# Order of the weight completion, pool order and operand temporaries in an attention and two-stage expert kernel on one core

## The chip, the cores and the metric

The kernel runs on one core of a Trainium2 chip. The metric is the device time of one execution, in microseconds (us). The core's engines are TensorE (PE, the matmuls), VectorE (DVE), ScalarE (ACT), GpSimd (POOL), and SyncE (SP), which here issues all DMAs in one queue, in order.

## The reference

Chunked attention with 8 memory slots, then two feed-forward stages on its 3072 output rows, all in fp32:

```
scores = scale * (q_c @ k_full.T); a = softmax(scores); x = a @ v_full      # B=4, H=8, S=768, D=64, chunks of 32
h = x @ w_in;  g = h * tanh(softplus(h));  x = g @ w_out                    # 3072x512 by 512x2048 by 2048x512
xn = x / sqrt(mean(x*x) + 1e-6) * rms_g
out = (silu(xn @ w_gate) * (xn @ w_val)) @ w_out2                           # 512x1536 twice, 1536x512
```

## The kernel before, in words

**Precision.** Every fp32 matrix is split into a high part and a low remainder. `split` (L145, L146) does it in two steps: ACT casts the high part (L145), then DVE subtracts it from the source (L146). Each product is then three matmuls (high by high, high by low, low by high: L612 to L614, L725 to L727, L854 to L856).

**Seven products for eight.** The stages w_in, gate/value and w_out2 form each 2x2 block product from seven products of sums of blocks, numbered 1 to 7 and run in the order 1, 6, 5, 4, 2, 7, 3 (`group`). Sums of the right operand's blocks are made on DVE in `sum_pieces` (L588 to L591, two of them into temporaries), then split one by one. Sums of a weight's blocks are made once: a weight of w_in that was first used with plain blocks is completed by `finish`, which adds high and low part back together on DVE (L273, two instructions for each weight), forms four sums on POOL (L278, L279) and DVE (L280, L281), and splits them into the remaining places of its slot.

**Stages.** Attention is interleaved with the w_in stage at the start: a block of 384 tokens that is ready is evacuated by ACT into `xb` (L516), and plain products of it (`unit`, evacuated by ACT at L662) keep PE busy until two blocks make a pair. From the second pair on the seven products are used. Results `g` go to `g_scratch` in HBM. The w_out stage reads `g_scratch` back through `Feed`: `load` brings a step's operand, `split` applies the activation (ACT, L753) and splits it; a step `s` calls `load(s+3)`, `split(s+3)`, `load(s+5)`. Three operands are split ahead of the loop. The weights of w_out arrive as raw fp32 (`raw`, L141) and are converted by ACT and DVE (L194, L197, L201, L202, L208). RMS normalisation and the gate/value stage (`group2`, results to `h_scratch`) follow, then the last stage, `group3`: 24 units (j, r), each of seven products of 18 matmuls with 256 columns. Its six weight slots `o2` are loaded by `w_load` (L124), its operands by `h_load` (L835) and `h_pieces`.

**Order.** A scheduler that simulates the program decides, from data dependences and buffers, in which order each engine's instructions stand; `pin` keeps an instruction in the order of the program text. Buffers come from pools that rotate. The pools `cp` (6 tiles of 1.5 KB for each partition), `gp` (5 of 3 KB) and `tp` (8 of 6 KB) are closed after the w_in stage, and the pools of the later stages, `gl` (4 KB), `c` (2 of 2 KB) and `t` (8 of 8 KB), take the same 72 KB. A late tile waits for whatever last used the bytes under it.

Where a row of the tables says `w`, `s`, `sm` or `raw`, it names the tile whose bytes are used, which can hold something else: the second unit's operands lie in weight slot 2 (`w<-h_scratch`).

Of the kernel before, what the change touches and what calls it, by code (L numbers as in the profile page):

```python
# [8 lines left out]
F32 = mybir.dt.float32  # L9
# [4 lines left out]
ALU = mybir.AluOpType  # L14
# [15 lines left out]
def tile_kernel(  # L30
# [15 lines left out]
    nc = tc.nc  # L46
# [36 lines left out]
    rawp = ctx.enter_context(tc.tile_pool(name="rawp", bufs=2))  # L83
    cap = ctx.enter_context(tc.tile_pool(name="cap", bufs=3))
    mid_stack = ExitStack()
    cp = mid_stack.enter_context(tc.tile_pool(name="cp", bufs=6))
    gp = mid_stack.enter_context(tc.tile_pool(name="gp", bufs=5))
    tp = mid_stack.enter_context(tc.tile_pool(name="tp", bufs=8))
    late_pools = {}
    psp = ctx.enter_context(tc.tile_pool(name="psp", bufs=1, space=bass.MemoryType.PSUM))  # L90
    bk = [psp.tile([128, 512], F32, name=f"bk{c}") for c in range(6)]
# [27 lines left out]
    def as7(s):  # L119
        return s.rearrange("p (a l f) -> p a l f", a=7, l=2)  # L120

    def w_load(key, u):
        s = w_slot(u)
        nc.sync.dma_start(out=s.bitcast(F32), in_=wd[key].bitcast(F32))  # L124
        wtab[key] = as7(s)

    def w_store(key, half):
# [140 lines left out]
    def finish(key):  # L268
        w = wtab[key]
        aa = [cap.tile([128, 512], F32, tag="ca", name="ca") for n in range(2)]  # L270
        for n, a in enumerate(aa):
            hi, lo = (w[:, 2 * n:2 * n + 2, l, :].bitcast(F32) for l in range(2))
            nc.vector.tensor_tensor(a.rearrange("p (a f) -> p a f", a=2), hi, lo, op=ALU.add)  # L273
        a0, a1 = aa
        a11, a12, a21, a22 = a0[:, 0:256], a0[:, 256:512], a1[:, 0:256], a1[:, 256:512]
        sm = cvp.tile([128, 4, 256], F32, tag="sm", name="sm")
        s4, s1, s2, s3 = (sm[:, i, :] for i in range(4))
        nc.gpsimd.tensor_tensor(s1, a21, a22, op=ALU.add)  # L278
        nc.gpsimd.tensor_tensor(s3, a11, a21, op=ALU.subtract)  # L279
        nc.vector.tensor_tensor(s2, s1, a11, op=ALU.subtract)  # L280
        nc.vector.tensor_tensor(s4, a12, s2, op=ALU.subtract)  # L281
        yield
        split(s4, w[:, 2, 0, :], w[:, 2, 1, :])
        yield
        split(sm[:, 1:4, :], w[:, 4:7, 0, :], w[:, 4:7, 1, :])
        yield
# [271 lines left out]
    def t_pieces(j, x0, x1, new, temp_new, dram, tab):  # L558

        return sum_pieces(j, x0[:, 0:2, :], x0[:, 2:4, :], x1[:, 0:2, :], x1[:, 2:4, :],  # L560
                          new, temp_new, dram, tab)

    def sum_pieces(j, b11, b21, b12, b22, new, temp_new, dram, tab):
        cols = b11.shape[2]
        size = b11.shape[1] * cols
        temp = {}

        def as_block(x):
            return x[:, 0:size].rearrange("p (a n) -> p a n", n=cols)

        def one(p, src):
            t = new()
            if isinstance(t, tuple):
                split(src, *t)
                for l in range(2):
                    store_later(dram[:, p - 1, l].bitcast(F32), t[l].bitcast(F32))
                return
            v = t.rearrange("p l a n -> p l (a n)")[:, :, 0:size]
            v = v.rearrange("p l (a n) -> p l a n", n=cols)
            split(src, v[:, 0], v[:, 1])  # L580
            if dram is not None:
                store_later(dram[:, p - 1].bitcast(F32), t.bitcast(F32))
            tab[j, p] = v

        def sums():
            for p in (2, 4):
                temp[p] = as_block(temp_new(p).rearrange("p a n -> p (a n)"))
            nc.vector.tensor_tensor(b11, b12, b11, op=ALU.subtract)  # L588
            nc.vector.tensor_tensor(temp[2], b22, b11, op=ALU.subtract)
            nc.vector.tensor_tensor(temp[4], temp[2], b21, op=ALU.subtract)  # L590
            nc.vector.tensor_tensor(b12, b22, b12, op=ALU.subtract)  # L591

        early = [lambda: one(1, b11), sums]
        rest = [lambda: one(6, temp[2]), lambda: one(5, b11), lambda: one(4, temp[4]),
                lambda: one(2, b21), lambda: one(7, b12), lambda: one(3, b22)]
        return early, rest

# [15 lines left out]
            nc.tensor.matmul(ps, whi, xl, start=False, stop=False, **more)  # L613
            nc.tensor.matmul(ps, wlo, xh, start=False, stop=kk == 1, **more)  # L614

    def group(mul, banks, n_, c12, c21, c22, temps):

        X, Y, Z, V = banks
        x, y, z, vv = (b_[:, 0:n_] for b_ in banks)
        s1, u2, z5 = temps()  # L620
        mul(1, X, True)
        nc.scalar.copy(s1, x)  # L622
        yield
        mul(6, Y, True)
        nc.vector.tensor_tensor(u2, y, s1, op=ALU.add)
        yield
        mul(5, Z, True)
        nc.scalar.copy(z5, z)
        yield
        mul(4, V, True)  # L630
        yield
        mul(2, X, False)
        yield
        mul(7, Y, False)
        u3 = s1
        nc.vector.tensor_tensor(u3, y, s1, op=ALU.add)  # L636
        yield
        mul(3, Z, False)
        nc.vector.tensor_tensor(c12, z, u2, op=ALU.add)
        nc.gpsimd.tensor_tensor(c22, u3, z5, op=ALU.add)  # L640
        nc.vector.scalar_tensor_tensor(
            c21, vv, -1.0, u3, op0=ALU.mult, op1=ALU.add
        )
        yield
# [194 lines left out]
        hraw[n] = parts  # L839

    def h_pieces(n):
        return sum_pieces(n, *hraw.pop(n), t_new2, v_temp, None, ttab_h)

    def group3(n, j, r, between):
        o = s_new()
        o = [o[:, a, :] for a in range(2)]

        def mul(p, bank_, first):
            t = ttab_h[n, p]
            ps = bank_[:, 0:256]  # L850
            more = dict(skip_group_check=not first)
            for f in range(HG):
                w = wtab["o2", f][:, W_AT[p]]
                nc.tensor.matmul(ps, t[:, 0, f], w[:, 0], start=first and f == 0, stop=False, **more)  # L854
                nc.tensor.matmul(ps, t[:, 0, f], w[:, 1], start=False, stop=False, **more)  # L855
                nc.tensor.matmul(ps, t[:, 1, f], w[:, 0], start=False, stop=f == HG - 1, **more)  # L856

        banks = group_banks(8)
        c11 = banks[0][:, 0:256]
        c12, c21, c22 = o[1][:, 0:256], o[0][:, 256:512], o[1][:, 256:512]  # L860
        run([group(mul, banks, 256, c12, c21, c22, lambda: (c_new()[:, 0:256], c12, c22))], between)
        nc.scalar.copy(o[0][:, 0:256], c11)
        for a in range(2):
            row = (2 * j + a) * N2 + 128 * r
            store_later(out[row:row + 128, :], o[a])
# [182 lines left out]
    late_pools["gl"] = late_pool("gl", 1)  # L1048
    late_pools["c"] = late_pool("c", 2)
    late_pools["t"] = late_pool("t", 8)  # L1050
    pend = []
    sq_new = lambda: [c_new() for _ in range(2)]
    for s, (m, i) in enumerate(steps):
# [106 lines left out]
    for jn, j in enumerate(jback):  # L1160
# [7 lines left out]
        for f in range(HG + 2 if jn else HG, F2):  # L1168
            run([group2(j, f)], preparing(0, bt) if last and f == F2 - 1 else bt)
            if last and f == HG + 2:  # L1170
                w_load(("o2", 3), 5)
            elif last and f == HG + 3:
                h_load(0, *units[0])
                w_load(("o2", 4), 6)
            elif last and f == HG + 4:
                w_load(("o2", 5), 3)
    h_load(1, *units[1])
    for n, (j, r) in enumerate(units):
        if 0 < n < len(units) - 1:
# [34 lines left out]
```

## Time and profile before

| | |
|---|---|
| median of the runs | 1191.08 us (1189.69 to 1196.43, 3 runs) |
| profiled execution | 1190.69 us, span 1188.9 us |
| mean granted clock of TensorE | 0.990 of full speed |
| busy: PE, DVE, ACT, POOL | 1153.8, 817.5, 621.5, 215.1 us |
| DMA, mean over the span | 247 GB/s |

The span runs from the first instruction to the last; the execution's own time holds the span and 1.8 us around it. Busy is the time in which an engine executes. PE's busy time includes stretches at the lower of its two clocks, so busy does not mean busy at full speed. An idle time is told with its releaser, the instruction whose end let the waiting one start.

### The profile page before, as it was taken

The page shows a single profiled execution, that of the slowest core. Times are in us where ns is not written, and L with a number is a line of the kernel's source. Part 1 is how long each engine was busy: PE and PEld are TensorE (multiplying, and loading weights), DVE is VectorE, ACT ScalarE, POOL GpSimd, SP SyncE. Part 2 cuts the span into 40 slices and gives each one's busy share as a digit, 9 for nine tenths or more (in the row PEclk, how much of TensorE's full clock was granted, in tenths as well). Part 3 has the DMA queues.
Part 4 walks back from the last instruction along what each step waited for, and adds up shares of the span by engine and source line. Part 5 has one row for each costly group of instructions (what it writes and reads, how often), then busy time and mean ns, then how long its engine had stood idle before and what let it go on. Part 6 is the DMA issues. An engine that isn't in the chain of part 4 may idle for free.

```text
span 1188.9 us, 22951 instructions
## 1 busy us (share of the span) xinstructions
PE 1153.8 (97%) x9052; PEld 1008.5 (85%) x9052; DVE 817.5 (69%) x1212; ACT 621.5 (52%) x996; POOL 215.1 (18%) x185
## 2 busy tenths in 40 slices
PE   6899899999999899999999999999999999999998
PEld 4789899999999688888878878878888888999998
DVE  4655898854755856675775675976886746887773
ACT  5566566543545866667665443553454423444442
POOL 2010222310132411030131121322221211000000
PEclk8899989999999999999999999999999999999999
DMA  9889869899488764595589388899889878654420
GB/s 188 172 230 217 209 239 264 231 293 300 148 304 289 246 204 129 187 362 163 195 329 393 144 343 333 321 416 391 319 312 377 315 264 293 195 173 142 142 90 36
DMA packets 219132, 294.20 MB, mean 247 GB/s; under 512 B 104208, under 2 KB 168720, under 8 KB 210064
## 3 DMA queue, kind: packets, MB, share of 16 engines
q1 hardware_dynamic: 219024, 292.73, 74.1%
q8 instruction: 71, 1.16, 0.4%
q14 instruction: 37, 0.30, 0.1%
HBM read 181.80 MB, written 110.89 MB: 246 GB/s over the span
## 4 chain that ended last, share of the span: by engine, by line
PE 74%; DMA 8%; DVE 7%; ACT 5%; issue 3%; POOL 2%; SPq 0%; ACTq 0%; POOLq 0%; DVEq 0%
PE bk L612 13%; PE bk L614 12%; PE bk L613 12%; DMA s<-g_scratch 4%; PE bk L856 4%; PE bk L854 4%; PE bk L855 4%; PE bk L726 3%; PE bk L727 3%; PE bk L725 3%; PE bkp L612 2%; PE bkp L614 2%; PE bkp L613 2%; PE bkp L434 2%; PE bkp L483 1%
## 5 line engine op out<-in xcount | busy, mean ns | idle before, releaser
L612 PE MATMUL bk<-T,w 128*128 128x384 f32 (+1 forms) x860 | 317.3, 372 | 5.5 <-ACT g L662 4.1
L613 PE MATMUL bk<-T,w 128*128 128x384 f32 (+1 forms) x860 | 312.5, 363 | 0.0
L614 PE MATMUL bk<-T,w 128*128 128x384 f32 (+1 forms) x860 | 311.6, 364 | 0.0
L612 PEld LDWEIGHTS bk<-T,w 128*128 128x128 f32 x860 | 162.7, 190 | 26.7 <-ACT g L662 4.3
L613 PEld LDWEIGHTS bk<-T,w 128*128 128x128 f32 x860 | 162.5, 189 | 17.3 <-issue 0.2
L614 PEld LDWEIGHTS bk<-T,w 128*128 128x128 f32 x860 | 162.3, 189 | 16.8
L854 PE MATMUL bk<-w,T 128*128 128x256 f32 x396 | 112.3, 284 | 2.9 <-ACT T L145 1.8
L725 PE MATMUL bk<-T,w 128*128 128x512 f32 x276 | 109.1, 396 | 2.9 <-ACT T L145 2.9
L856 PE MATMUL bk<-w,T 128*128 128x256 f32 x396 | 111.4, 282 | 0.2 <-DVE T L146 0.2
L855 PE MATMUL bk<-w,T 128*128 128x256 f32 x396 | 111.4, 281 | 0.0
L726 PE MATMUL bk<-T,w 128*128 128x512 f32 x276 | 109.4, 396 | 0.3 <-DVE T L146 0.3
L727 PE MATMUL bk<-T,w 128*128 128x512 f32 x276 | 108.6, 393 | 0.0
L640 POOL TENSOR_TENSOR v<-c,v 128x512 f32<-128x512 f32 x36 | 51.6, 1436 | 222.3 <-DVE c L636 164.8
L636 DVE TENSOR_TENSOR c<-bk,c 128x512 f32<-128x512 f32 (+2 forms) x72 | 43.1, 599 | 63.4 <-PE bk L614 51.7
L622 ACT COPY c<-bk 128x512 f32<-128x512 f32 (+2 forms) x72 | 37.0, 516 | 83.9 <-PE bk L614 33.3
L146 DVE TENSOR_TENSOR T<-s,T 128x1024 fp32r<-128x1024 f32 (+1 forms) x50 | 61.3, 1235 | 26.0 <-ACT T L145 25.5
L854 PEld LDWEIGHTS bk<-w,T 128*128 128x128 f32 x396 | 75.2, 190 | 4.2 <-ACT T L145 2.9
L855 PEld LDWEIGHTS bk<-w,T 128*128 128x128 f32 x396 | 75.5, 191 | 0.1
L856 PEld LDWEIGHTS bk<-w,T 128*128 128x128 f32 x396 | 75.0, 190 | 0.4 <-DVE T L146 0.4
L753 ACT ACTIVATE s<-s 128x1024 f32<-128x1024 f32 x44 | 46.7, 1061 | 38.6 <-DMA s<-g_scratch 36.6
L725 PEld LDWEIGHTS bk<-T,w 128*128 128x128 f32 x276 | 51.8, 188 | 15.4 <-ACT T L145 3.3
L726 PEld LDWEIGHTS bk<-T,w 128*128 128x128 f32 x276 | 52.0, 188 | 13.2 <-issue 1.2
(218 smaller groups left out, 2309.2 us busy)
## 6 DMA issues: line engine op xcount, KB each, us to landing
T<-nt_scratch SPq DMA_DIRECT2D x35, 1024.0 KB
g_scratch<-g SPq DMA_DIRECT2D x64, 384.0 KB
s<-g_scratch SPq DMA_DIRECT2D x46, 512.0 KB
h_scratch<-s SPq DMA_DIRECT2D x36, 512.0 KB
w<-wg SPq DMA_DIRECT2D x10, 1792.0 KB
wg<-w SPq DMA_DIRECT2D x30, 512.0 KB
raw<-in_moe_w_out_dram SPq DMA_DIRECT2D x28, 512.0 KB
nt_scratch<-T SPq DMA_DIRECT2D x14, 1024.0 KB
```

What stands on the lines that cost most here:

```text
L146: keep((eng or nc.vector).tensor_tensor(lo, src, hi.bitcast(F32), op=ALU.subtract))
L612: nc.tensor.matmul(ps, whi, xh, start=first and kk == 0, stop=False, **more)
L613: nc.tensor.matmul(ps, whi, xl, start=False, stop=False, **more)
L614: nc.tensor.matmul(ps, wlo, xh, start=False, stop=kk == 1, **more)
L640: nc.gpsimd.tensor_tensor(c22, u3, z5, op=ALU.add)
L725: nc.tensor.matmul(ps, ahi, bhi, start=start, stop=False)
L726: nc.tensor.matmul(ps, ahi, blo, start=False, stop=False)
L727: nc.tensor.matmul(ps, alo, bhi, start=False, stop=stop)
L753: nc.scalar.activation(x, g, self.act)
L854: nc.tensor.matmul(ps, t[:, 0, f], w[:, 0], start=first and f == 0, stop=False, **more)
L855: nc.tensor.matmul(ps, t[:, 0, f], w[:, 1], start=False, stop=False, **more)
L856: nc.tensor.matmul(ps, t[:, 1, f], w[:, 0], start=False, stop=f == HG - 1, **more)
```

## The change

1. In `finish`, the two DVE sums of high and low part are pinned to program order for the weight slots 6 and 5.
2. The pools that are closed after the w_in stage are opened in another order: `tp`, `gp`, `cp` instead of `cp`, `gp`, `tp`. So the late pools lie over other tiles than before.
3. The fourth operand of the w_out stage is split ahead of the loop (`feed.split(4)`).
4. `w_load` can cut its transfer. The load of the sixth `o2` slot, 1792 KB, becomes three transfers: one seventh, three sevenths, three sevenths (the columns of product 1, of products 2 to 4, of products 5 to 7, by the slot's places).
5. `h_pieces` no longer uses temporaries: differences are formed in place, in the block that is no longer needed, just before their split. For this product 5 comes before product 6 in `group3`, both in the preparation and in the matmuls.

```diff
+    tp = mid_stack.enter_context(tc.tile_pool(name="tp", bufs=8))
+    gp = mid_stack.enter_context(tc.tile_pool(name="gp", bufs=5))
     cp = mid_stack.enter_context(tc.tile_pool(name="cp", bufs=6))
-    gp = mid_stack.enter_context(tc.tile_pool(name="gp", bufs=5))
-    tp = mid_stack.enter_context(tc.tile_pool(name="tp", bufs=8))
...
-    def w_load(key, u):
+    def w_load(key, u, cuts=()):
         s = w_slot(u)
-        nc.sync.dma_start(out=s.bitcast(F32), in_=wd[key].bitcast(F32))
+        edges = (0,) + cuts + (7,)
+        for a, b in zip(edges, edges[1:]):
+            at = slice(512 * a, 512 * b)
+            nc.sync.dma_start(out=s[:, at].bitcast(F32), in_=wd[key][:, at].bitcast(F32))
...
-            nc.vector.tensor_tensor(a.rearrange("p (a f) -> p a f", a=2), hi, lo, op=ALU.add)
+            ins = nc.vector.tensor_tensor(a.rearrange("p (a f) -> p a f", a=2), hi, lo, op=ALU.add)
+            if key[1] in (6, 5):
+                pin(ins)
...
-        mul(6, Y, True)
-        nc.vector.tensor_tensor(u2, y, s1, op=ALU.add)
-        yield
-        mul(5, Z, True)
-        nc.scalar.copy(z5, z)
-        yield
+        for p in (5, 6) if five_first else (6, 5):
+            if p == 6:
+                mul(6, Y, True)
+                nc.vector.tensor_tensor(u2, y, s1, op=ALU.add)
+            else:
+                mul(5, Z, True)
+                nc.scalar.copy(z5, z)
+            yield
...
     def h_pieces(n):
-        return sum_pieces(n, *hraw.pop(n), t_new2, v_temp, None, ttab_h)
+        b11, b21, b12, b22 = hraw.pop(n)
+        one = lambda p, src: sum_one(n, p, src, t_new2, None, ttab_h)
+        sub = lambda out, a, b: nc.vector.tensor_tensor(out, a, b, op=ALU.subtract)
+        early = [lambda: one(1, b11), lambda: sub(b11, b12, b11), lambda: sub(b12, b22, b12)]
+
+        def p5():
+            one(5, b11)
+            sub(b11, b22, b11)
+
+        def p6():
+            one(6, b11)
+            sub(b11, b11, b21)
+
+        return early, [p5, p6, lambda: one(2, b21), lambda: one(4, b11),
+                       lambda: one(7, b12), lambda: one(3, b22)]
...
+    feed.split(4)
...
-                w_load(("o2", 5), 3)
+                w_load(("o2", 5), 3, (1, 4))
```

`sum_one` is the former inner function `one` of `sum_pieces` (split, and a later store where there is one), moved out so that both callers share it. In `group3` the group is called with `five_first=True`.

What the scheduler makes of it shows at three places. First VectorE, where the second pair's operand sums (L588 to L591) are made, just before the w_in stage switches to seven products. `ca<-w` are the sums of `finish`, `kw` holds keys of the attention, `sm` the block sums of a weight. Before:

```order
L273 TENSOR_TENSOR ca<-w 128x512
L280 TENSOR_TENSOR sm<-sm,ca 128x256
L281 TENSOR_TENSOR sm<-ca,sm 128x256
L273 TENSOR_TENSOR ca<-w 128x512 x2
L146 TENSOR_TENSOR w<-sm,w 128x3x256
L387 COPY kw<-bk_87 128x16x8
L146 TENSOR_TENSOR w<-sm,w 128x256
L588 TENSOR_TENSOR xb<-xb 128x768
L387 COPY kw<-kw 128x16x8
L589 TENSOR_TENSOR g<-xb 128x768
L591 TENSOR_TENSOR xb<-xb 128x768
L590 TENSOR_TENSOR g<-g,xb 128x768
```

The changed kernel at the same place (its line numbers are its own: L276 is the old L273, L285 and L286 are L280 and L281, L149 is L146, L392 is L387, L597 to L600 are L588 to L591):

```order
L285 TENSOR_TENSOR sm<-sm,ca 128x256
L286 TENSOR_TENSOR sm<-ca,sm 128x256
L149 TENSOR_TENSOR w<-sm,w 128x3x256
L392 COPY kw<-bk_87 128x16x8
L149 TENSOR_TENSOR w<-sm,w 128x256
L392 COPY kw<-kw 128x16x8
L597 TENSOR_TENSOR xb<-xb 128x768
L598 TENSOR_TENSOR g<-xb 128x768
L600 TENSOR_TENSOR xb<-xb 128x768
L599 TENSOR_TENSOR g<-g,xb 128x768
```

Three sums `ca<-w` have left the stretch ahead of the operand sums and, like the sums of the next slot, stand behind the pair's six operand splits; one copy of `kw` now stands ahead of both operand sums. POOL's sums L278 and L279, which need `ca`, move behind with them.

Second ScalarE, at the switch from the w_in to the w_out stage. `T<-sm` is the split of the first operand that goes into a tile of the late pool `t`; `ca`, `lr` and `w<-ca` belong to the conversion of raw weights. Before:

```order
L197 ACTIVATE lr<-raw 128x512
L753 ACTIVATE sm<-w 128x1024
L194 ACTIVATE ca<-raw 128x512
L145 CAST w<-ca 128x512
L197 ACTIVATE lr<-raw 128x512
L145 CAST w<-ca 128x512
L145 CAST T<-sm 128x1024
```

The changed kernel (L764 is the old L753, L148 is L145, L200 is L197, L197 is L194):

```order
L200 ACTIVATE lr<-raw 128x512
L764 ACTIVATE sm<-w 128x1024
L148 CAST w<-ca 128x512
L148 CAST T<-sm 128x1024
L197 ACTIVATE ca<-raw 128x512
L200 ACTIVATE lr<-raw 128x512
```

The split `T<-sm` stands one cast behind the activation that makes its source, and one conversion of a raw weight has moved behind it. Before, its tile lay over tiles of `gp` that were still being stored; now it lies over a tile of `tp`, and it waits for the last matmul that read that tile.

Third the DMA queue, at the switch from gate/value to the last stage. Before:

```order
L124 DMA w<-wo 128x3584
L110 DMA h_scratch<-s 128x1024
L835 DMA raw<-h_scratch 128x6x128
L835 DMA raw<-h_scratch 128x6x128
L835 DMA sm<-h_scratch 128x6x128
L835 DMA s<-h_scratch 128x6x128
L835 DMA w<-h_scratch 128x6x128
L835 DMA w<-h_scratch 128x6x128
```

The changed kernel (L846 is the old L835, L127 is L124):

```order
L846 DMA raw<-h_scratch 128x6x128
L127 DMA w<-wo 128x512
L127 DMA w<-wo 128x1536
L127 DMA w<-wo 128x1536
L846 DMA raw<-h_scratch 128x6x128
L110 DMA h_scratch<-s 128x1024
L846 DMA sm<-h_scratch 128x6x128
L846 DMA w<-h_scratch 128x6x128
L846 DMA w<-h_scratch 128x6x128
```

The cut load now stands behind one load of the third unit's operands (`raw`), and the second unit's operands (`w<-h_scratch`) stand ahead of the load into `s`. On PE the last product of gate/value that reads weight slot 2 has moved from the middle of the first unit's fourth product to within its first product.

## Rows read from the trace of the kernel before

**Rows 1.** The page: span, and busy us (share) xinstructions of each engine.
```profile
span 1188.9 us, 22951 instructions
PE 1153.8 (97%) x9052; PEld 1008.5 (85%) x9052; DVE 817.5 (69%) x1212; ACT 621.5 (52%) x996; POOL 215.1 (18%) x185
```

**Rows 2.** PE's waits from 140 to 1100 us: total us, times, longest.
```profile
PE bk L612 <- ACT g L662: 4.1, 1, 4.1
PE bk L725 <- ACT T L145: 2.9, 1, 2.9
PE bk L854 <- ACT T L145: 1.8, 3, 1.0
...
PE bk L854 <- DMA w<-wo: 1.0, 1, 1.0
```

**Rows 3.** Windows: stretch, us, busy us of each engine, granted clock, DMA share.
```profile
148.08:154.91 6.83, 6.14 (x72) 5.21 (x72) 6.83 (x12) 6.83 (x14) 0.00 (x0) 0.50 0.95 374
...
397.25:400.67 3.42, 3.42 (x9) 2.65 (x9) 3.39 (x5) 3.42 (x5) 0.00 (x0) 0.50 0.43 142
...
700.00:985.00 285.00, 284.22 (x1241) 232.54 (x1240) 206.01 (x304) 123.22 (x224) 62.63 (x53) 1.00 0.90 342
...
1030.00:1188.90 158.90, 155.56 (x1305) 155.36 (x1303) 115.83 (x151) 65.80 (x100) 12.32 (x11) 1.00 0.41 124
```

**Rows 4.** Timeline of VectorE, 140 to 149 us: start, us, instruction, idle before.
```profile
140.00 0.69 DVE L273 TENSOR_TENSOR ca<-w 128x512 f32<-128x512 f32 x1
...
141.40 1.28 DVE L273 TENSOR_TENSOR ca<-w 128x512 f32<-128x512 f32 x2
142.61 0.95 DVE L146 TENSOR_TENSOR w<-sm,w 128x768 fp32r<-128x768 f32 x1
...
144.46 0.94 DVE L588 TENSOR_TENSOR xb<-xb 128x768 f32<-128x768 f32 x1
145.32 0.74 DVE L387 COPY kw<-kw 128x128 f32<-128x128 f32 x1
145.99 1.49 DVE L589 TENSOR_TENSOR g<-xb 128x768 f32<-128x768 f32 x1
```

**Rows 5.** Timeline of ScalarE, 147 to 149 us.
```profile
147.51 0.83 ACT L145 CAST T<-g 128x768 fp32r<-128x768 f32 x1 [3.98 <-DVE g L589]
148.25 0.47 ACT L662 COPY g<-bk 128x384 f32<-128x384 f32 x1
```

**Rows 6.** Timeline of TensorE, 144 to 149 us.
```profile
148.77 0.69 PE L612 MATMUL bk<-T,w 128*128 128x384 f32 x1 [4.07 <-ACT g L662]
```

**Rows 7.** Timeline of GpSimd, 144 to 147 us.
```profile
144.68 1.30 POOL L278 TENSOR_TENSOR sm<-ca 128x256 f32<-128x256 f32 x1 [0.42 <-DVE w L146]
```

**Rows 8.** Chain that ended last, 385 to 400 us: start, us, what.
```profile
390.32 4.28 DMA g_scratch<-g
```

**Rows 9.** Timeline of VectorE, 388 to 396 us.
```profile
388.56 0.85 DVE L208 CUSTOM_DVE_ANT_0 ca<-ca,lr 128x1024 uint16<-128x1024 uint16 x1
```

**Rows 10.** Timeline of ScalarE, 394 to 396 us.
```profile
394.70 1.05 ACT L145 CAST T<-sm 128x1024 fp32r<-128x1024 f32 x1 [0.94 <-DMA g_scratch<-g]
```

**Rows 11.** Timeline of TensorE, 997 to 1004 us.
```profile
997.75 0.28 PE L854 MATMUL bk<-w,T 128*128 128x256 f32 x1
...
1003.13 0.39 PE L854 MATMUL bk<-w,T 128*128 128x256 f32 x1 [0.97 <-DMA w<-wo]
```

**Rows 12.** Chain that ended last, 980 to 1026 us.
```profile
996.13 6.96 DMA w<-wo
...
1010.77 4.23 DMA w<-h_scratch
1015.02 0.84 ACT T L145
...
1018.96 1.50 DVE w L591
```

**Rows 13.** Timeline of SP's queue, 985 to 1020 us: DMA issues.
```profile
1010.77 3.14 SPq L835 DMA_DIRECT2D w<-h_scratch  x4
```

More of the change, by code (lines that the diff above doesn't have):

```diff
@@ L561, in t_pieces, with sum_one @@
                           new, temp_new, dram, tab)
+    def sum_one(j, p, src, new, dram, tab):
+        cols = src.shape[2]
+        size = src.shape[1] * cols
+        t = new()
+        if isinstance(t, tuple):
+            split(src, *t)
+            for l in range(2):
+                store_later(dram[:, p - 1, l].bitcast(F32), t[l].bitcast(F32))
+            return
+        v = t.rearrange("p l a n -> p l (a n)")[:, :, 0:size]
+        v = v.rearrange("p l (a n) -> p l a n", n=cols)
+        split(src, v[:, 0], v[:, 1])
+        if dram is not None:
+            store_later(dram[:, p - 1].bitcast(F32), t.bitcast(F32))
+        tab[j, p] = v
     def sum_pieces(j, b11, b21, b12, b22, new, temp_new, dram, tab):
@@ L569, in as_block @@
             return x[:, 0:size].rearrange("p (a n) -> p a n", n=cols)
[L571 to L583, printed above, removed]
+        one = lambda p, src: sum_one(j, p, src, new, dram, tab)
         def sums():
@@ L614, in product, with group @@
             nc.tensor.matmul(ps, wlo, xh, start=False, stop=kk == 1, **more)
-    def group(mul, banks, n_, c12, c21, c22, temps):
+    def group(mul, banks, n_, c12, c21, c22, temps, five_first=False):
         X, Y, Z, V = banks
@@ L860, in group3 @@
         c12, c21, c22 = o[1][:, 0:256], o[0][:, 256:512], o[1][:, 256:512]
-        run([group(mul, banks, 256, c12, c21, c22, lambda: (c_new()[:, 0:256], c12, c22))], between)
+        run([group(mul, banks, 256, c12, c21, c22, lambda: (c_new()[:, 0:256], c12, c22),
+                   True)], between)
         nc.scalar.copy(o[0][:, 0:256], c11)
```

## The prediction

> **What bounds the kernel now.** I read the page first. PE is busy 1153.8 us of a span of 1188.9 [rows 1], so everything that can be won without taking matmuls away lies in the other 35 us and in stretches in which PE runs at its lower clock. The list of PE's waits comes next: the reader is to see that from 140 us on four entries stand out, 4.1 us for an evacuation of ACT at L662, 2.9 us and 1.8 us for casts of operands on ACT, 1.0 us for the load of a weight [rows 2]. Most of the rest of the 35 us lies in the start-up, where the change moves nothing, and in the last 3.3 us (158.90 less 155.56, the last window [rows 3]); shorter waits stand in stages that it leaves alone. The windows then tell what the clock adds: twice PE runs at half of full speed, 1.2 instead of 2.4 GHz, for 6.83 us from 148.08 and for 3.42 us from 397.25 [rows 3], both times behind one of the two long waits. What was done in 6.14 and 3.42 us of busy time there takes half at full clock, so the first stretch costs 3.1 us and the second 1.7. The three places are called A (about 145), B (about 393) and C (about 1001 to 1023).
>
> **The change at A: sums behind the operand sums.** PE waits 4.07 us until 148.77 [rows 6] for the evacuation at 148.25, which stands in ACT's queue behind the cast of 147.51, and that cast waits 3.98 us for the DVE sum L589 [rows 5]. L589 starts at 145.99, at the end of an unbroken row of DVE work [rows 4]. Two things are taken from in front of it. Three of the L273 sums: by the starts of what follows, the first is worth about 0.60 us (its 0.69 overlaps the next by 0.09) and the pair 142.61 - 141.40 = 1.21, together 1.81. And L589 itself took 1.49 us where its neighbour L588, of the same shape, took 0.94 [rows 4]; L278 of POOL ran beside it from 144.68, with a successor of its kind behind it [rows 7], and POOL's pair needs the moved sums, so it now runs later. That is up to 0.55 us. Together 2.36 at most. I take 2.2, since the copy of `kw` now stands ahead of both sums and L588 still waits for the block's evacuation; lower bound 1.8, the sums alone. The wait shrinks from 4.07 to about 1.9 us; it does not vanish. For the clock I have rows on both sides: behind 4.07 us of wait the stretch at half clock was 6.83 us long, behind 2.9 us it was 3.42, and behind the waits of C, at most 1.05 us each, the granted clock stayed full. A wait of 1.9 us lies between; I take one stretch of 3.42, which leaves a gain of 3.1 - 1.7 = 1.4, with bounds 0 and 3.1.
>
> The work is not gone: the sums and what follows them (L280, L281, L278, L279, split) now stand behind six operand splits, and completing the weights of slots 6 and 5 comes later, by some 6 us for the first. Queued behind them on DVE are the combines of the pair's first groups and the copies of attention; the one that waits is PE, at the first product of the weight of slot 6 that needs a sum. Following the new order with the durations of the rows, that weight is complete a bit under a microsecond before PE wants it. I put 0.5 us against it, bounds 0 and 2.
>
> **B: pools and the fourth split.** PE waits 2.87 us, until 395.80, for the split of the first operand that lies in a late tile. Its cast at 394.70 waits for a store of `g` that was issued at 390.32 and landed 4.28 us later [rows 8, 10]: the tile lay over `gp`. In the new layout it lies over a tile of `tp` whose last reader on PE is long past. What the cast then waits for is its place in ACT's queue: one cast ahead of it needs the DVE step L208, which ends at 388.56 + 0.85 = 389.41 [rows 9]. With 0.6 for that cast (0.83 for 768 columns [rows 5], so 0.55 for 512) the split starts at 390.0, its cast ends at 391.1 (1.05 [rows 10]), and the subtraction on DVE (0.94 for 768 columns [rows 4], so 1.25 for 1024) at 392.3, before PE ran dry at about 392.9 (2.87 ahead of 395.8). The wait vanishes, and with it the half-clock stretch: 2.87 + 1.7 = 4.6. Only some 0.6 us of cover remains, so a lower bound is 2.9: half of the wait stays without a change of clock (1.4 + 1.5). The conversions and loads put behind the split are wanted some 6 us later than they come, so I give them no price.
>
> **C: the cut load and operands in place.** Here PE waits 1.0 us for the load of the sixth `o2` slot and 1.8 us in three pieces for casts [rows 2], 2.8 in all. The load is issued at 996.13 and lands 6.96 us later [rows 12], and the matmul that needs it runs at 1003.13 [rows 11]. In the new order product 1 needs only the first seventh. Ahead of it in the queue now stands a `raw` load (384 KB), which waits for a DVE subtraction that I place at 994.9, so the pieces are still issued at about 996.1. The third piece is first needed after 12 matmuls of 512 columns and 39 of 256 behind 997.75 [rows 11], at 0.23 each (284.22 / 1241) and 0.12 (155.56 / 1305 [rows 3]): 2.7 + 4.6, so at 1005.1. If the pieces share the queue as one transfer does, it lands at 996.13 + 6.96 = 1003.1, or about 1.5 later if the whole `raw` load goes first (384 of 1792 KB, by 6.96): in time either way, just.
>
> The Trainium skill, page "DMA: Bandwidth & Descriptors", section "Anatomy of one DMA", speaks against cutting: each DMA costs about 2.0 us that do not scale with its size, besides its bytes at 436 GB/s (a fit for another issue path than this queue's). As an estimate by that page, three pieces end to end take 2.6 + 3.8 + 3.8 = 10.2 us, the last lands at 1006.3, and C would gain 1.2 us less. The trace bears out the fixed part only for DMAs that stand alone: four loads of 384 KB were issued within 3.14 us [rows 13], and the operand was there 4.23 us after the first [rows 12], so pieces overlap, and I go by that.
>
> The second unit's operands hang on weight slot 2. Before, its last reader ran up to 1010.5, the loads went out at 1010.77 and PE's casts followed from 1015.02, through L591 with 1.50 us beside POOL [rows 12]. Now that reader stands in the first unit's first product and ends at about 1002, so the loads go out some 8 us earlier; the waits at 1020 to 1023 (1.3 of the 1.8) go. I take 2.3 for C: bounds 0 (the queue's new head holds the load back as long as the wait it saves) and 2.8.
>
> **The later units.** Their instructions are as many as before; PE runs 155.56 of 158.90 us there without a wait, with ACT busy for 65.80 and DVE for 115.83 [rows 3]. Differences in place put a serial chain on DVE and ACT: cast 0.84 [rows 12], subtraction for the split and difference about 0.95 each, 2.7 us for products 5 and 6, less for the others, which have no difference behind them; some 14 us for a unit of 126 matmuls by 0.12 = 15.0 us if nothing overlaps, and the casts do. I price it at nothing; cover is the spare operand tiles that hold a unit's work ahead of PE.
>
> **Sum.** 2.2 + 1.4 - 0.5 + 4.6 + 2.3 = 10.0 us from the profiled execution's 1190.69 gives 1180.7. That execution is 0.4 below the median of the runs, so the forecast is 1180.7 to 1181; I write 1180.8. Its own range: best 2.36 + 3.1 + 4.6 + 2.8 = 12.9, so 1177.8; worst 1.8 + 0 - 2 + 2.9 + 0 = 2.7, but not all at once; two of three at the lower bounds give about 1186.
>
> **The rivals.**
> - *The wait at A moves to the completed weight.* DVE works without a break from 140 us on, and the moved work stands at the end of it. If the weight of slot 6 comes 2 us or more late, with a half-clock stretch as behind the 2.9 us wait, A returns nothing: 4.6 + 2.3 = 6.9, so 1183.8. For it: the thin lead. Against it: five of the combines in between need PE first, so DVE is not the only pacemaker. Chance 0.17.
> - *The change doesn't do what it says at B.* The operand's split escapes the stores, but another tile of the group still lies over `g`, or the earlier fourth split takes ACT's time just then, and PE still waits as long. Then 10.0 - 4.6 = 5.4: 1185.3. For it: 0.6 us of cover. Against it: the stores land at 394.6, and the operands over them are wanted two steps later. Chance 0.13.
> - *Slower: the in-place chain paces the last stage.* If a unit's operands take longer than its 15.0 us of matmuls, each of some 22 units adds the excess: the operand tiles come free in PE's order, the DVE chain waits for them, and POOL's combines lengthen sums from 0.95 to 1.50 [rows 12]. It decides from 0.75 us for a unit on, where 16 us are lost and 10 gained: 1197. Against it: DVE is free for 43 of 158.9 us there and ACT for 93 [rows 3]. Chance 0.06.
>
> **How the numbers follow.** Forecast 0.64 and the three rivals make one. Half a per cent, 6 us, is about what a measurement of this kernel can tell from no change: its three runs lie 0.57% apart. Faster by more than that needs a time under 1185.1: the forecast nearly whole (0.61), the first rival mostly (0.14), the second less than half (0.05), so 0.80; slower 0.05; within, 0.15. The range is 1177 to 1186.5: below it only an undercounted clock, above it part of the second rival and the third, some 2 in 10 together.
>
> **What would show it.** At A: `T<-g` cast about 2 us earlier, PE idle of 1.7 to 2.3 us there, the half-clock window shorter than 6.83 us, no new PE wait for `w` splits near 158. At B: no wait of L725 for a cast near 393, no half clock at 397. At C: no wait for `w<-wo`, `w<-h_scratch` issued near 1002, the casts of the second unit ahead of its matmuls. After 1030 the window's PE share unchanged. The prediction is wrong if DVE's backlog reaches PE, or if time won at A is lost again before 390 to a load that cannot come earlier.

## The result and the profile after

The changed kernel takes 1179.97 us (median of 6 runs, 1174.78 to 1183.14) where the kernel before takes 1190.67 (6 runs, 1188.47 to 1196.43): 0.990 of its time, 95% interval 0.9868 to 0.9931. The forecast was 1180.8 in a range from 1177.0 to 1186.5. The profiled execution took 1180.75 us with a span of 1178.9. In the experiments below, one execution of 2873 us (of the kernel with parts 2 and 3) lies far outside all others and is left out of its median and its ratio. The page of the changed kernel begins:

```profile
span 1178.9 us, 22945 instructions
PE 1149.5 (98%) x9052; PEld 1005.6 (85%) x9052; DVE 816.9 (69%) x1212; ACT 619.9 (53%) x996; POOL 212.7 (18%) x185
```

The span is 10.0 us shorter and PE's busy time 4.3 us shorter than in [rows 1], with the same number of matmuls: about 6 us of idle time went, and 4 us in which PE was busy but slow. The list of PE's waits (line, what it waited for, total us, times, longest) shows which of the four entries of [rows 2] are left:

```profile
PE bk L621 <- ACT g L673: 1.9, 1, 1.9
PE bk L621 <- DVE c L647: 1.8, 2, 1.0
PE bkp L621 <- DVE v L652: 1.2, 1, 1.2
...
PE bk L621 <- ACT c L639: 0.6, 1, 0.6
PE bk L471 <- ACT p L458: 0.5, 1, 0.5
PE bk L621 <- ACT g L709: 0.2, 1, 0.2
```

L621 is the old L612, L673 the old L662. The first entry fell from 4.1 to 1.9; those at B and C are gone. New are the one of ACT `p` (a step of the attention), the one of ACT `g` at L709, and the 1.0 us of DVE `c`, where before there was one wait of 0.8. The windows (us, busy us of PE, its weight loads, DVE, ACT, POOL, granted clock, DMA share, GB/s) tell the rest:

```profile
147.97:155.00 7.03, 7.03 (x93) 5.40 (x94) 6.29 (x9) 6.79 (x13) 0.00 (x0) 1.00 1.07 384
391.00:400.00 9.00, 9.00 (x40) 7.32 (x39) 8.97 (x12) 6.65 (x9) 1.56 (x1) 1.00 0.65 211
...
985.00:1018.00 33.00, 33.00 (x239) 31.26 (x238) 24.50 (x33) 13.63 (x21) 3.33 (x3) 1.00 0.76 244
1018.00:1178.90 160.90, 157.35 (x1320) 157.15 (x1318) 120.01 (x154) 65.11 (x100) 10.25 (x11) 1.00 0.42 125
```

Both stretches at half clock of [rows 3] now run at 1.00. From 985 to 1018 PE is busy without a break, and in the last stage it leaves out 3.55 us, about as much as before (162.90 less 159.56 from 1026 on in the trace before, 3.3).

**Reading a change place by place.** Two executions differ by some us in the start-up, which the change does not touch. So I compare traces by the lead: the start of a matmul (the n-th of its stage) in one trace, less its start in the trace of before. Negative is ahead. What happens at a place is the change of the lead across it. For the changed kernel the lead is +1.4 at 144 us (times of the trace before), -2.8 at 160, -0.8 at 372 and 386, -6.0 at 405, -5.6 at 984, and -10.2 from 1030 to the end. So it lost 1.4 us in the start-up, won 4.2 at A and gave 2.2 of that back by 254, won 5.2 at B and 4.6 at C; between 405 and 984 it lost 0.4.

At A the timelines of VectorE, ScalarE and TensorE (start, us, instruction, idle time before it) now read:

```profile
144.74 0.95 DVE L597 TENSOR_TENSOR xb<-xb 128x768 f32<-128x768 f32 x1
145.72 0.96 DVE L598 TENSOR_TENSOR g<-xb 128x768 f32<-128x768 f32 x1
```
```profile
146.71 0.83 ACT L148 CAST T<-g 128x768 fp32r<-128x768 f32 x1 [2.46 <-DVE g L598]
147.44 0.47 ACT L673 COPY g<-bk 128x384 f32<-128x384 f32 x1
```
```profile
147.97 0.44 PE L621 MATMUL bk<-T,w 128*128 128x384 f32 x1 [1.86 <-ACT g L673]
```

The chain is that of [rows 4 to 6], shorter by the sums, and the second operand sum takes 0.96 us where L589 took 1.49: POOL's pair L278 and L279 no longer runs there. Before, L279 ran beside L589, from 145.94 to 146.66; L278 had ended at 145.98, when L589 began, and had itself taken 1.30 us beside L588, which took its usual 0.94.

### The profile page after: what moved, and what is told of

The parts are those of the page before. It is cut to its first block, busy times and chain, and to the rows that moved or that the text cites. A ratio compares the mean times of both kernels' runs of the same rounds, so it can differ in the third digit from the quotient of the medians.

```text
span 1178.9 us, 22945 instructions
## 1 busy us (share of the span) xinstructions
PE 1149.5 (98%) x9052; PEld 1005.6 (85%) x9052; DVE 816.9 (69%) x1212; ACT 619.9 (53%) x996; POOL 212.7 (18%) x185
## 4 chain that ended last, share of the span: by engine, by line
PE 74%; DVE 8%; DMA 8%; ACT 5%; issue 2%; POOL 2%; SPq 1%; ACTq 0%; DVEq 0%
PE bk L621 13%; PE bk L623 12%; PE bk L622 12%; PE bk L879 4%; PE bk L880 4%; PE bk L881 4%; PE bk L737 3%; PE bk L738 3%; PE bk L736 3%; DMA s<-g_scratch 3%; DMA raw<-in_moe_w_in_dram 2%; PE bkp L621 2%; PE bkp L623 2%; PE bkp L622 2%; PE bkp L439 1%
## 5 line engine op out<-in xcount | busy, mean ns | idle before, releaser
L621 PE MATMUL bk<-T,w 128*128 128x384 f32 (+1 forms) x860 | 315.9, 370 | 5.0 <-ACT g L673 1.9
L621 PEld LDWEIGHTS bk<-T,w 128*128 128x128 f32 x860 | 161.7, 188 | 26.4 <-DVE c L647 2.7
L149 DVE TENSOR_TENSOR T<-s,T 128x1024 fp32r<-128x1024 f32 (+1 forms) x50 | 61.1, 1232 | 29.9 <-ACT T L148 29.4
L764 ACT ACTIVATE s<-s 128x1024 f32<-128x1024 f32 x44 | 46.6, 1060 | 36.8 <-DMA s<-g_scratch 32.7
L737 PEld LDWEIGHTS bk<-T,w 128*128 128x128 f32 x276 | 51.8, 188 | 12.4 <-issue 1.2
```

What stands on the lines that cost most here:

```text
L149: keep((eng or nc.vector).tensor_tensor(lo, src, hi.bitcast(F32), op=ALU.subtract))
L621: nc.tensor.matmul(ps, whi, xh, start=first and kk == 0, stop=False, **more)
L737: nc.tensor.matmul(ps, ahi, blo, start=False, stop=False)
L764: nc.scalar.activation(x, g, self.act)
```

## The experiments

In the tables of changes of the lead below, A is from 144 to 372 us, B from 386 to 405, C from 984 to 1030, all in times of the trace before, each from one profiled execution. A minus sign is time won. Line numbers are each kernel's own.

**Pools and fourth split: pin alone, pools alone, split alone, both.** Each of the first four kernels is the kernel before with one part, or two, of the change.

```diff
# pin alone: in finish
+            if key[1] in (6, 5):
+                pin(ins)
# pools alone: order of opening
+    tp = mid_stack.enter_context(tc.tile_pool(name="tp", bufs=8))
     gp = mid_stack.enter_context(tc.tile_pool(name="gp", bufs=5))
+    cp = mid_stack.enter_context(tc.tile_pool(name="cp", bufs=6))
# split4 alone: after the late pools
+    feed.split(4)
```

> Only part 1: the sums of weight slots 6 and 5 pinned behind the operand sums; the rest as before. Theory (each place pays for itself, A nets about 2 us): the wait of L612 for the evacuation L662 near 148 falls from 4.07 to 1.8-2.0 us, no half clock behind it, but new waits of together 1 to 2 us appear between 155 and 245 (attention and combines behind the moved sums); gain over the kernel before 1.5 to 3 us, the waits near 393 and 1001-1023 unchanged. Rival (the moved sums cost nothing and the waits at 181 and 235 of the changed kernel came from the different start-up of that execution): no waits over 0.3 us between 155 and 245, gain 4.5 to 5.5 us.

> Only part 2: the order of the three pools. Theory (the place of the split in ScalarE's queue matters as much as the bytes under its tile): the first late operand no longer waits for a store of g, but it still stands behind a second converted weight, whose cast needs VectorE's step that ended at 393.1; so PE's wait near 393 falls from 2.9 to about 1.9 us, the half-clock stretch may stay; gain 0.9 to 2.6 us. Rival (the pool order alone carries place B): wait gone, gain 4.6 us or more.

> Only part 3: the fourth operand split ahead of the loop. Theory: its tile still lies over the stores of g, so the cast waits for the same store as before; PE's wait near 393 stays at 2.5 to 3 us, gain 0 (within 0.5 us at that place). Rival (ScalarE's queue was the limit and the store only the last name on it): wait under 1 us, gain over 3 us.

> Parts 2 and 3 together. Theory: wait near 393 gone with the half-clock stretch behind it, 4.6 to 5.3 us gained there, nothing elsewhere; so the two parts give together 2 us or more above the sum of each alone. Rival (the two add up or one carries all): the gain is that of pools alone within 0.5 us.

> Parts 2 and 3 together, as before in this study, for its profile (the one taken then was of an execution of 2873 us among five of 1184.5 to 1186.0, and tells nothing of the waits). Theory: no wait of L725 for a cast near 393 and full clock behind it, the fourth-product wait near 148 and the waits at 1001 to 1023 as in the kernel before; the lead over the kernel before grows by 4.6 to 5.3 us between 373 and 404. Rival (B was won by something else in the changed kernel): the wait stays above 1 us.

| kernel | time, median | ratio to before | A | B | C |
|---|---|---|---|---|---|
| pin alone | 1188.48 | 0.9987 (0.9968 to 1.0006) | -3.4 | -2.4 | +1.3 |
| pools alone | 1192.29 | 1.0015 (0.9995 to 1.0036) | -0.5 | -2.3 | -0.2 |
| split4 alone | 1188.16 | 1.0003 (0.9984 to 1.0022) | -1.1 | 0.0 | +0.9 |
| pools and split4 | 1184.95 | 0.9965 (0.9952 to 0.9977) | -0.5 | -5.2 | +0.6 |

The places of the last row are those of the second run of that kernel. The medians tell only that kernel from no change; the intervals of the three single parts hold 1, so what follows on them rests on the places, one execution each. ScalarE's timelines at B tell why neither part does it alone. With the fourth split alone:

```profile
389.29 0.62 ACT L145 CAST w<-ca 128x512 fp32r<-128x512 f32 x1 [0.64 <-DVE ca L208]
394.75 1.04 ACT L145 CAST T<-sm 128x1024 fp32r<-128x1024 f32 x1 [4.84 <-DMA g_scratch<-g]
```

The operand's cast stands right behind the first converted weight, and waits 4.84 us for the store. With the pools alone:

```profile
390.53 0.62 ACT L145 CAST w<-ca 128x512 fp32r<-128x512 f32 x1 [2.40 <-DVE ca L208]
391.05 1.04 ACT L145 CAST T<-sm 128x1024 fp32r<-128x1024 f32 x1
```

The store is out of the way, but ScalarE waits 2.40 us in front of a second converted weight, and the operand's cast stands behind that; PE's wait falls to 1.83 us. With both:

```profile
390.24 0.62 ACT L145 CAST w<-ca 128x512 fp32r<-128x512 f32 x1 [0.65 <-DVE ca L208]
390.76 1.05 ACT L145 CAST T<-sm 128x1024 fp32r<-128x1024 f32 x1
```

and PE does not wait. So B had two limits one behind the other, and the fourth split, called for nothing but one more operand, takes the second away. The 2.3 us of the pools alone may not be credited to them: the kernel with the last stage alone changed (in place, six first, below) shows the same timeline in an execution whose store landed in 2.95 us instead of the 4.28 of [rows 8], and won 2.35 at B with nothing changed there, and the pin alone won 2.38 with a store of 3.09. In the execution of the pools alone the store had landed at 390.99, just ahead of the cast, so it would hardly have been in the way in the old layout either. What the pools are worth shows when both parts are in: in all five profiles with both, the cast starts 2.9 to 4.4 us before that store lands (by its semaphore); without the pools it never does.

The pin's wait at 148 fell to 2.06 us at full clock, as expected. The rival (the moved sums cost nothing) is out: between 160 and 254 the lead fell by 1.1 us, with PE waits of 0.41 and 0.20 at 179 and 190, together less than the 1 to 2 us that the theory expected. Part of the rest went at 383, in this execution (the second fence is ScalarE's, the third the window behind the wait, with the columns of above):

```profile
383.01 0.44 PE L614 MATMUL bk<-T,w 128*128 128x384 f32 x1 [1.99 <-ACT c L630]
```
```profile
381.54 1.06 ACT L755 ACTIVATE sm<-w 128x1024 f32<-128x1024 f32 x1 [3.12 <-DMA w<-g_scratch]
382.50 0.46 ACT L630 COPY c<-bk 128x384 f32<-128x384 f32 x1
```
```profile
384.13:387.54 3.41, 3.41 (x10) 2.64 (x9) 3.41 (x5) 3.15 (x6) 3.04 (x2) 0.50 0.48 123
```

An evacuation that PE waits for stands on ScalarE behind the activation of an operand that a DMA brings, and behind this wait of 1.99 us PE ran 3.41 us at half clock. The 1.3 us that the pin alone lost at C, and the 0.9 of the split alone, go with another stretch of 3.41 us at half clock, near 1000, which the other executions do not show there.

**Place C: in place alone, cut alone, the product order alone, and the two apart.**

```diff
# in place alone: h_pieces without temporaries, five_first in group3; the load in one piece
# cut alone:
+                w_load(("o2", 5), 3, (1, 4))
# five first only: temporaries kept
+        early, rest = sum_pieces(n, *hraw.pop(n), t_new2, v_temp, None, ttab_h)
+        return early, [rest[1], rest[0]] + rest[2:]      # and five_first in group3
# in place, six first: h_pieces as changed, group3 without five_first
```

> Only part 5: differences in place, product 5 ahead of 6; the sixth slot of the last stage is loaded in one piece. Theory (the order of the queue carries the cast waits, the cut carries the load's wait): the four waits for casts at 1001 and 1020 to 1023 vanish, but the load stands behind a load of raw and lands later, so PE's wait for it stays or grows, 0.8 to 2.3 us; the lead between 985 and 1030 grows by 2.3 to 3.8 us; after 1030 nothing changes. Rival 1 (in place alone carries place C): no wait for the load, 4.3 us or more. Rival 2 (the serial chain in place paces the last stage): the lead shrinks steadily after 1030.

> Only part 4: the load of the sixth slot cut in three. Theory: PE's wait of 1.0 us for that load vanishes, and the waits for casts at 1001 and 1020 to 1023 stay as they are or take over a part of it; the lead between 985 and 1030 grows by 0.5 to 1.2 us. Rival (pieces cost more than they save: each carries a fixed time of its own, so the third lands later than the whole did): a new wait of 0.5 us or more for the second or third piece, and a lead of 0 or less.

> The kernel before with only the product order of the last stage changed, 5 ahead of 6 in the preparation and in the matmuls; the temporaries stay. Theory (the in-place differences, not the product order, let the scheduler end gate/value early and so free weight slot 2): the second unit's loads still go out near 1010, the waits at 1020 to 1023 stay; the lead between 985 and 1030 changes by less than 1 us. Rival (the order alone does it): loads near 1002, lead of 4 us or more.

> The kernel before with the differences in place, prepared in the order 1, 5, 6, 2, 4, 7, 3, but with the matmuls of the last stage in the old order, 6 ahead of 5. Theory (place C is won by the in-place preparation, which ends gate/value early and frees weight slot 2; the matmul order only gives PE more work to put ahead of the late slot): the second unit's loads go out near 1000 to 1002 and the waits at 1020 to 1023 are gone; a wait of up to 1 us for the load of the sixth slot or for product 6's cast can remain; the lead between 985 and 1030 grows by 3.3 to 4.6 us. Rival (both orders must agree): waits of 1 us or more for casts, lead under 2.5 us.

| kernel | time | A | B | C | after 1030 | second unit's loads issued from |
|---|---|---|---|---|---|---|
| in place alone | 1184.59, ratio 0.9934 (0.9908 to 0.9960) | -1.4 | 0.0 | -4.6 | 0.0 | 1000.80 |
| cut alone | 1191.05, ratio 0.9990 (0.9978 to 1.0002) | -0.9 | -0.1 | +0.3 | 0.0 | 1009.27 |
| five first only | 1186.45, one run | -1.5 | -0.2 | -2.2 | 0.0 | 1008.58 |
| in place, six first | 1185.30, one run | -0.5 | -2.4 | -3.3 | 0.0 | 999.94 |

Before, these loads went out at 1010.77 [rows 13]. My theory fell here: in place alone carries the whole of C in its execution, load included, and the cut alone gives nothing. Cut alone, PE no longer waits for the load, but the waits for operands take its place (PE's waits from 985 to 1030):

```profile
PE bk L857 <- ACT T L148: 2.0, 4, 1.0
PE bk L859 <- DVE T L149: 0.9, 2, 0.7
PE bkp L857 <- ACT T L148: 0.2, 1, 0.2
```

In place alone there is no wait from 985 to 1030 at all. Its instruction order on PE shows why the whole load comes in time: 24 matmuls of products 5 and 6 now stand between the last matmul of product 1 that needs another slot and the first that needs the late one, 24 by 0.12 = 2.9 us, because their operands are ready. By its semaphore the load landed 7.1 us behind its issue, and PE wanted it 9.0 behind. Both halves of the in-place change have a share. With the product order alone the loads of the second unit still go out at 1008.6, and waits of 0.9 and 0.4 us for their operands stay; the theory expected less than 1 us from it, and it won 2.2. With the in-place preparation but product 6 first, the second unit's waits are gone and the load's is back:

```profile
1004.23 0.39 PE L877 MATMUL bk<-w,T 128*128 128x256 f32 x1 [1.10 <-DMA w<-wo]
```

**The changed kernel again, without the cut, without the pin.**

> The changed kernel itself, for a second profile and beside its two relatives on one chip. Theory: the places repeat (wait near 148 of 1.8 to 2.1 us with full clock behind it, none near 393, none at 1001 to 1023); the wait of 0.99 us at 235 of its first profile was of that execution and does not come back, the ones of 0.4 to 0.5 and 0.2 us at 181 and 192 do. If it then reaches 372 us with a lead over 2 us, the evacuation near 384 waits longer than the 0.6 us of the first profile (behind the operand that ScalarE has to take from memory first): 1 to 2 us. Gain in time 9 to 13 us. Rival: the waits at 181 to 235 all come back and are the price of the moved sums.

> The changed kernel with the sixth slot loaded in one piece again. Theory (what in place alone showed: PE has other products to run before it needs that slot): no wait for the load, the lead between 985 and 1030 grows by 4.4 to 4.7 us as in the changed kernel, and the time is the changed kernel's within 2 us. Rival (in the changed kernel PE is ahead of the queue by more, so the cut is needed): a wait of 0.5 us or more for the load.

> The changed kernel without part 1. Theory: the wait near 148 is back at 3.9 to 4.1 us with a half-clock stretch behind it, no waits between 155 and 245, places B and C as in the changed kernel; 2 to 3 us slower than the changed kernel. Rival 1 (what the pin wins is given back in full before the w_out stage): the same time within 1 us. Rival 2 (the pin is worth its whole 5 us): 4.5 us slower or more.

```diff
# without the cut
-                w_load(("o2", 5), 3, (1, 4))
+                w_load(("o2", 5), 3)
# without the pin
-            if key[1] in (6, 5):
-                pin(ins)
```

| kernel | time, median | ratio to before | at 144 | 144 to 160 | 160 to 254 | A | B | C | whole |
|---|---|---|---|---|---|---|---|---|---|
| changed, first profile | 1179.97 | 0.9900 (0.9868 to 0.9931) | +1.4 | -4.2 | +2.2 | -2.2 | -5.2 | -4.6 | -10.2 |
| changed, again | 1179.01 | 0.9905 (0.9885 to 0.9926) | +0.3 | -4.5 | +1.1 | -3.8 | -5.2 | -4.6 | -12.4 |
| without cut | 1177.24 | 0.9901 (0.9877 to 0.9925) | -2.5 | -4.2 | +1.1 | -3.5 | -5.3 | -3.2 | -15.4 |
| without pin | 1181.21 | 0.9922 (0.9903 to 0.9941) | -0.8 | -1.0 | 0.0 | -0.9 | -5.2 | -4.6 | -11.1 |

The wait of 0.99 us at 235 did not come back in the second profile, so it belonged to the first execution; those of ACT `p` and of `g` did (0.55 and 0.19 us at 180 and 191), and they are missing without the pin. ScalarE in that second profile tells what passes the first of them on:

```profile
176.32 1.28 ACT L148 CAST w<-sm 128x768 fp32r<-128x768 f32 x2 [1.67 <-DVE sm L285]
...
178.88 0.63 ACT L458 ACTIVATE p<-p 128x512 f32<-128x512 f32 x1
```

The activation `p` stands in an unbroken row of ScalarE's work that begins with the cast of a weight's block sums, and that cast waits for L285, a block sum of `finish`, at the end of a row in which VectorE shows no idle time since 158.37. Without the cut there is one wait for the load at C, 0.83 us:

```profile
993.93 0.38 PE L879 MATMUL bk<-w,T 128*128 128x256 f32 x1 [0.83 <-DMA w<-wo]
```
```profile
983.92 9.97 DMA w<-wo
```

and C wins 1.4 us less, as the rival expected, though PE's order there is that of in place alone, where the load came in time. The rival's reason does not hold: in both executions the load is issued 2.98 us ahead of the first unit's first matmul, so PE is not further ahead of the queue. What differs is the landing (the second fence, from the chain that ended last): 9.97 us behind the issue, against 7.1. In place with six first it took 10.2 us, in six other profiles with a whole load 6.9 to 7.2; in the four profiles with the cut the last piece landed 7.2 to 7.6 us behind the first issue. Why the load was late in two executions is open; in both, a load into `raw` had been issued 0.8 to 1.2 us ahead of it, and 2.0 us ahead in place alone. So the cut is worth 0 to 1.4 us at its place, by how the whole load happens to run; in the medians it does not show (1177.24 without, 1179.01 with, intervals that overlap). Without the pin the wait near 148 is back:

```profile
148.10 0.45 PE L619 MATMUL bk<-T,w 128*128 128x384 f32 x1 [3.86 <-ACT g L671]
```

and A wins 0.9 us instead of 2.2 to 3.8. Beside each other on one chip the medians put the pin at 2.2 us (1181.21 less 1179.01), which fits the expectation of 2 to 3; the leads put it at 1.3 to 3.0, and the pin alone came out at 1.5 with an interval that holds no change. Without the pin the medians won 9.7 us against the kernel before, and B and C together are 9.8. The expected wait of 1 to 2 us near 384 at a large lead did not come either: 0.41 and 0.35 us at leads of 3.5 and 6.0. So the 1.99 us of the pin alone was a load that came late in that execution: the activation behind it started 6.0 us after the load's issue, in four other profiles 4.1 to 4.6.

## Why the prediction was right, point by point

**The time** was right to 0.8 us, and that is in part luck. The terms of B and C were too small by 0.6 and 2.3 us, that of A too large by about 0.8 (below), and in the profiled execution the start-up cost 1.4. By places the change is worth about 12 us (2.3 + 5.2 + 4.6) where the sum has 10.0; the medians of the first comparison gave 10.7, those of the second 11.9. The list of waits in the prediction also leaves out one of 1.0 us for DVE `v`, as long as its fourth entry; the change left it standing (1.2 after).

**A, the wait.** Right: 4.07 to 1.86 us, about 1.9 forecast, by both ways named; the sums went from in front and L598 ran beside nothing on POOL, though what had run beside L589 was L279, not the L278 of the prediction. **A, the clock.** I took one stretch at half clock behind the shorter wait. There was none: the four profiles with the pin show waits of 1.57 to 2.06 us and the granted clock at 1.00. That is what these four did, and not sure for a wait of that length: behind the 1.99 us at 383 the pin alone did run 3.41 us at half clock. The loss of before was also less sure than one trace shows: behind waits of 3.86 to 4.07 us, the kernels without the pin show a stretch of 6.83 us in some executions and of 3.41 in others. Taken together, the lead from 144 to 160 grew by 4.0 to 4.5 us in the four with the pin and by 0.2 to 1.1 in the eight without; 4.23 - 0.79 = 3.4 by their means, against 3.6 forecast.

**A, the give-back.** Mis-sized: 0.5 us forecast, 1.1 measured in three profiles and 2.2 in one, of which 1 us was the wait at 235. It also came elsewhere: PE never waited for the weight of slot 6, but for a step of the attention at 180, behind the late weight sums, and an evacuation at 191, which only the kernels with the pin show; what passes that one on is not traced. The net of A was 2.2 to 3.8 against 3.1 forecast, but only against a trace of before that had the long stretch at half clock: the eight kernels without the pin also won 0.5 to 1.5 us there. By the means the pin is worth 3.2 - 0.9 = 2.3, so the term was 0.8 too large.

**B.** Right in place and mechanism, 5.2 us in all four kernels with both parts against 4.6. The step that was a little short: after the first wait the trace before holds a second of 0.29 us, for the subtraction of the same operand, which I left out, and a wait costs more than its idle time (next point). That the fourth split was needed for it I did not see; I credited the pools and read the shorter queue on ScalarE from the order without asking which part had made it.

**C.** The term was mis-sized and in part credited to the wrong part: 2.3 us forecast with 2.8 as its bound, 4.6 measured in four of the five profiles with the differences in place and product 5 first (the fifth is the one without the cut where the load came late). I counted the idle times that the waits list. But here each wait cost more than its idle time. The trace before, TensorE:

```profile
1020.92 0.28 PE L855 MATMUL bk<-w,T 128*128 128x256 f32 x1
1022.24 0.39 PE L854 MATMUL bk<-w,T 128*128 128x256 f32 x1 [1.05 <-ACT T L145]
1022.47 0.28 PE L855 MATMUL bk<-w,T 128*128 128x256 f32 x1
...
1023.13 0.28 PE L854 MATMUL bk<-w,T 128*128 128x256 f32 x1
1023.25 0.28 PE L855 MATMUL bk<-w,T 128*128 128x256 f32 x1
```

Undisturbed, matmuls overlap: each takes 0.28 us by the profile and the next starts 0.12 behind it (the last two lines). Across the wait it is 1.32 us from start to start, of which the idle time counts only 1.05, since the 0.28 us of the matmul in front run out alone; and the matmul that waited is followed after 0.23. In the trace before, twelve matmuls from 997 to 1030 are followed by more than the usual distance, together 4.61 us beyond it, while their idle times come to 2.98. That is the whole of what C won. And the load needed cutting less than I thought: the new order on PE hid the whole load in one of two executions without the cut.

In the changed kernel the pieces were issued from 990.50 on. By its semaphore the third had landed 7.4 us later, within the 7.0 to 8.5 of the prediction; PE used it at 999.5, 9.0 us behind the first issue, and did not wait:

```profile
990.50 1.27 SPq L127 DMA_DIRECT2D w<-wo  x3
...
996.50 5.71 SPq L846 DMA_DIRECT2D w<-h_scratch  x4
```

So here they overlapped: together they took hardly longer than the 7.0 us of the whole load before. The four loads of [rows 13] had overlapped too, but the 4.23 us that the prediction reads from [rows 12] is the landing of the first of them; the last landed 8.1 us behind the first issue. The Trainium skill's figure for a fixed cost of each DMA (page "DMA: Bandwidth & Descriptors", section "Anatomy of one DMA", a fit for another issue path) had given an estimate of 10.2 us if the pieces ran end to end, and the trace does not agree. The second line of the fence is the second unit's load, 14.3 us earlier than in [rows 13], of which 5.6 are the lead at 984; that leaves 8.6 for the 8 us of the prediction.

**The later units.** Right: the lead does not move by 0.05 us after 1030 in any of the profiles. **The rivals.** The wait at A did move, but only by the 1 to 2 us above; B did what it said; the in-place chain paces nothing.

## What to carry to other kernels

The idle time in front of a matmul can understate what a wait costs, as at C, where 2.98 us of idle time were 4.61; compare the distances between matmuls with those of an undisturbed stretch, and add the clock behind it. A wait can have a second limit right behind the first, as at B, where buffer and queue had to be changed together: look what stands in front of the late instruction once its named releaser is gone. And where executions differ more than the parts of a change, compare traces place by place by the lead of the same matmul; single parts of 2 us that the medians could not tell stood out there. But take several executions for a place too: one trace of before had the longer of two losses at A, and a store that landed early won 2.4 us at B with nothing changed.

## What the runs showed that was not expected

The start-up, the same instructions in all of these kernels, differs by up to 4.2 us between executions (the lead at 144 us ran from -2.5 to +1.7 in the twelve profiles that show it). How much of the spread of the times it makes is not shown, since only profiled executions tell it. TensorE's lower clock behind one and the same wait lasted 6.83 us in some executions and 3.41 in others; behind waits of 2.1 us and less at A it did not come, but it came, for 3.41 us each time, behind the 1.99 us at 383 of the pin alone, and in two executions (pin alone, split4 alone) near 1000, around two waits of 0.57 and 1.1 us that follow each other. The pools alone had the same two waits there, 0.58 and 1.15 us, and kept full clock.
